# A fused attention and gated long convolution: two weight chunks moved ahead of two value tiles, and another order of work

## The chip, the cores and the metric

The kernel runs on one core of a Trainium2 chip. The metric is the device time of one execution in microseconds (us). Five executions of the kernel before took 173.39 to 174.32 us, median 173.7 us. One further execution was recorded by the hardware profiler; its numbers are the "profile" below.

The engines of the core are named as the profile names them: PE (the matrix engine, with PEld for its weight loads), DVE (VectorE), ACT (ScalarE), POOL (GpSimd) and SP (SyncE). Here POOL and SP do little but issue transfers, each in its own queue.

## The reference, cut to what matters

```python
def _attn_ref(q, k, v, n_global, n_local):           # 4 x 8 heads x 768 x 64, n_global 8, n_local 96
    scores = scale * np.matmul(q, k.transpose(0, 1, 3, 2))
    keep = is_global | is_local                      # the first 8 keys, or the last 96 positions
    scores = scores - slopes[:, None, None] * dist   # slopes 2 ** -(h + 1)
    scores = np.where(keep, scores, -1000000000.0)
    a = np.exp(scores - np.max(scores, axis=-1, keepdims=True))
    return np.matmul(a / (np.sum(a, axis=-1, keepdims=True) + 1e-09), v)

def _moe_ref(x, w_proj, filter_fft, w_out):          # x: 4 x 768 x 512, the attention's output
    proj = x @ w_proj                                # 512 x 1536
    x1, x2, x3 = (proj[..., :D], proj[..., D:2 * D], proj[..., 2 * D:])
    X2 = np.fft.rfft(x2, n=S, axis=1)
    H = np.fft.rfft(filter_fft, n=S, axis=0)[None, :, :]
    x2_conv = np.fft.irfft(X2 * H, n=S, axis=1)
    return (x1 * x2_conv * x3) @ w_out
```

Inputs and output are float32; the work is done in 16-bit types.

## The kernel before

**The work of one batch.** Attention is done in seven key tiles of 120 rows, collected in three groups `c` (tiles 0-1, 2-3, 4-6), with the eight heads in four pairs `hp`, and the pairs in two halves `j`. `scores` (L963) makes one PE group per pair and group; ACT turns it into `E` with an exponential (L1000). In batch 0 the bias and the mask are added by extra matmuls; in batches 1 to 3 DVE multiplies by a mask (L1007). `values` (L1010) multiplies `E` by the value tiles `vn`; DVE takes the reciprocal of the sums and scales the result into `xn`. `transpose_x` (L1059) turns `xn` by PE and copies it to `xT`. `values(j, 2)` needs the value tiles 3 to 6, those of the groups before it only lower ones. `gate` (L1098) makes x1 and x3 for one quarter of the 512 columns and one half `s` of the rows: two groups of four matmuls each, named w0 to w3 (x1) and w8 to w11 (x3) by their column block of `w_proj`. The half `s=0` needs `xT` of the groups 0 and 1 only; `s=1` needs group 2.

The convolution over 768 positions is split by hand into small transforms. `butterfly` (L1077) sums and subtracts thirds of `xT` on DVE, `proj` (L1169) multiplies them by the x2 columns, `spectra` (L1271) and `forward` (L915) transform the results, DVE multiplies by the filter's spectrum, PE does the inverse (L1191), DVE joins the parts (`mixed`, `gated`) and multiplies by x1*x3 to `y`, and `project` (L1219) multiplies by `w_out`. The result is evacuated into one of six buffers `ot` and stored by SP. Before the first convolution the tables of the transform and the filter's spectrum `h` are made too (`tables`, `spectrum`).

**What sets the order.** The kernel records all operations in a `Plan`, with a cost per engine and what each reads and writes. `lay` (L156) is a list scheduler in Python: of the operations that can start first it takes the one of lowest rank. The rank is the batch's due time, plus a bias, plus a noise number read from `NUDGES`, one per operation. An operation that ACT or DVE may do is given to the engine whose finish, by these costs, is earlier, after a lean has been added on DVE's side: `FAVOUR` plus a second number of `NUDGES`. So an entry of `NUDGES` can change both where an operation stands and who does it.

```python
e, s = min(((e, max(at, free[e])) for e in o.cost),
           key=lambda x: (x[1] + o.cost[x[0]] + o.lean * (x[0] == "V"), x[0]))
```

The costs serve only to fix the order. On the chip each engine works through its own list in that order, and semaphores make it wait for what it needs. Where the plan has a gap on PE, `fill` puts idle matmuls there (`busy`, L561) on a bank that is free.

**Transfers.** POOL issues all loads of q, k, v, `w_proj`, the filter and `w_out`, in the order of the recorded loads. For batch 0 `load_first` (L1313) issues the pairs of heads of q and k, then the seven value tiles, then `w_proj` in five chunks, then the filter:

```python
WL = None, None, None, [(0, 256), (1024, 256), (256, 256), (1280, 256), (512, 512)]
...
for t in range(7):
    self.load_run(("vn", 0), vt, self.v, t, 1)
for o in self.WL[3]:
    self.load_w(*o)
```

A chunk is named by its first column: w0 holds x1 of the blocks 0 and 1, w1024 x3 of the same, w256 and w1280 those of the blocks 2 and 3, w512 all of x2. The first pair of heads is loaded by SP in float32 into two buffers used later for something else (`ot` and `h1`, in `load_pair`, L600 to L616) and cast to 16 bits from there.

Of the kernel before, what the change touches and what calls it, by code (L numbers as in the profile page):

```python
# [64 lines left out]
class Plan:  # L65
# [90 lines left out]
    def lay(self):  # L156
# [84 lines left out]
        -20469, -15907, -15519, -41330, 21271, -19125, 0, -18788, -21220, 6002, 0, -7189, -43575, -36799,  # L241
        -6571, -28916, -3333, 19757, 53969, -12046, 3924, 2362, -27887, 22407, 12912, 8466, 24818, 892,
        -43717, 690, 23057, -7424, 0, -18348, 0, 12132, 0, 3318, 0, 307, 0, 10665, -36412, 26238, -3364,
        -7981, 0, 19285, 0, -5291, 0, -3358, -40138, 46, 0, 4893, -20410, 607, -3897, 25935, 14236, -472,
        -26253, 50953, -18333, -20987, 21604, -2252, -14900, -32001, -12177, 7553, 28609, 17506, -3743,
        -23847, 42942, 14917, 23914, 13863, -24322, 6302, -15137, -1614, -4820, -17466, 50019, 19029,
        -20858, -16941, -5845, 16570, 18752, -3067, 4401, 8349, 30366, -26959, 2604, 7945, 41591, -12869, 0,
        6221, 0, 17527, 0, -11888, 0, -33773, 0, -20135, 0, 31381, 0, 9598, 0, 342, 0, 5902, 0, 21318, 0,
        -31048, 0, 3779, 0, 7500, -33102, -3367, 7292, 574, -14517, -22474, 40989, -11563, -11866, -18943,
        21835, -13606, -7933, -12166, -5061, 14482, -66705, -16499, -72333, -45183, 18666, 14455, -1721,  # L250
        -14094, 21975, -16214, -38799, 11592, -32806, -4486, 58753, 1604, 32067, 9824, 58288, -8039, -6267,
        -7799, -30465, 16245, 29129, 47615, 14049, 20581, 7542, 9071, -14063, 1398, -21731, 17235, 5237,
        -5501, -11743, 11491, -6405, -6106, -51905, 13315, -17948, 16276, 5723, 510, -57089, 50036, 18885,
        10758, 3744, 17086, -20876, -6224, -59669, 34319, 11575, -10851, -49437, 16614, 3748, -6997, -23517,
        -741, -9617, -2158, -25727, 15549, -42179, 2206, 15498, 22052, 14638, 31730, -36475, -366, -1041,
        483, -60527, 26470, -25753, 48694, -36466, 4435, 25064, 15798, -2003, 880, 41085, 8640, 19549,
        -13373, 62494, -20031, -35301, -365, -10682, 12515, -39995, 9179, -44839, 20791, 21607, 12677,
        -8056, 11463, -7753, 23778, -7196, -828, 9869, 42664, -4575, 5499, -21685, -1123, 58706, -13769,
        1071, 15224, 31737, 4557, -51402, 30473, 10683, 37011, -21708, -22082, -18146, 13758, 35600, -13459,
        13377, 42708, 8338, 10228, -2747, -44553, -22549, 2967, -13095, -1261, -20387, 7291, -5928, 8626,  # L260
        -3903, -15574, 7036, -15402, -21901, 5357, -4808, 8631, -43985, -23660, 52225, -23, -37277, 3239,
        4765, 25180, -24965, -30489, -48437, 1398, 17933, -10027, 3345, -14007, -42685, -274, -8683, 11605,
        -32563, -13448, 31461, 27188, 5094, 5241, 42373, 5599, -31270, 5970, 9726, -15345, 27804, 10360,
        12837, -37873, 40504, 5471, 45899, 30654, -30112, -11882, 6890, -10173, 11360, -20642, 71457, -7037,
        37670, 35836, 15212, -3001, -161, -21054, 29167, -19964, -4626, 33026, -65921, 5985, -58627, -537,
        15188, 27998, -9214, -10266, -12514, 5532, -31329, -13816, -42538, -361, 42096, 9128, -53101,
        -24252, 36726, -6808, -39007, -15537, -38689, -36629, -7459, 13790, -6734, 1466, -11773, 3029,
        -61137, -5278, -32143, -4629, -16151, 28035, -11602, -28288, -20732, -10425, -9594, -25686, 22828,
        7308, 10617, 8409, -34612, 6321, 5099, 10385, -16522, -10028, 17262, -3342, 364, -17974, -61950,
        6074, 1677, -2070, 22933, -10718, 4341, -9076, -14027, -7023, -49231, 39984, 41324, -15930, 87908,  # L270
        29952, 30259, -1085, 17673, 22547, 65315, 11679, 71123, -10221, 17535, 4265, 30002, 38971, 52458,
        17154, 19646, 7993, -19925, 6995, 21573, 7611, 16678, 19381, -3732, -949, 89358, 14752, 32456,
        22564, 38857, 8243, 38484, 4106, 43844, 16240, 18442, 24005, 52322, -701, 54120, 10351, 816, -1700,
        36760, 14579, 12398, 35622, -18870, 13272, -8238, 15305, -14220, 3173, -10015, -12163, 21169, 18317,
        43800, 33470, -15626, -25950, 6510, 17663, 41448, -25293, -2107, 3876, 28549, 11063, 32221, 7491,
        20524, -12468, 39460, 3459, 30644, 28397, -32823, -23657, 9318, -14232, 4503, 30321, -4786, 9073, 0,
        47530, 0, 14649, 0, -6931, 0, 10167, 0, -22564, 27505, 17477, 0, -21831, -18775, 29130, 12351,
        -11426, 0, -23648, 0, -498, 0, -18653, 0, 20206, 0, -14460, 0, 5069, 0, -5644, 0, 17568, 0, -28141,
        0, -393, 0, -13744, 0, -23077, 0, 27342, 0, -17530, 0, 24883, -5429, -15687, 22286, 6382, -7868,
        14844, 27493, 22854, -7734, -7159, 20555, 20588, -3284, -9355, 45908, 26090, -1576, 10937, -27579,  # L280
        -21718, -32176, 45033, -3052, -19219, 33129, 27434, -1137, -11810, -13329, -2566, 2545, 4486,
        -15611, -1075, 9151, 352, -14471, 31815, -23667, -3395, 32969, -1271, 12653, 1976, 23324, -5368,
        -47352, 15491, 4886, 9690, 3559, 14583, 29188, 2353, 34301, 4910, 19200, -11179, 62728, 26450, 2457,
        -13343, 34676, 8057, -18974, -12923, -16321, -14742, 3933, 10896, -19278, 10205, 17364, -10269,
        16177, 35168, -20658, -11589, 43724, 41480, 24103, 858, 9853, 10552, 1525, -3996, -5471, 25781,
        30000, 2124, -2069, 21452, 930, 8726, 90512, 29611, -16321, -22500, 9310, 12752, 2100, 1887, -64324,
        -32791, -10156, 1195, -8986, 20032, 2698, -22611, 3783, -1678, 18174, -28792, -28897, -1554, 44027,
        3299, -48940, 4565, -18590, -16364, 3358, -7004, -1749, -3117, -99997, -7283, -11740, -961, 12244,
        3976, -41870, -15548, -14790, 16082, 20959, 12982, -28661, -9869, 11604, 34716, 7633, 8897, -35715,
        -33194, -11677, 21392, 27263, 20593, -24154, -8400, -33341, 33983, -5328, 3810, 16086, -23990,  # L290
        -15413, 7796, -4785, -18200, -31986, 960, -8033, 20448, 12322, -12111, -5519, -1954, -30857, -23631,
        -49557, 32119, 2870, 4580, 13819, 10505, -65607, 37080, -32639, 43079, -11814, -10582, -35676, 9162,
        -17164, 18890, 8216, -36193, -26951, 3373, 10331, 33775, -22565, 15472, -54239, 4898, -13691, 13051,
        -24460, -38679, -31280, 19957, -34749, -14184, -69485, 11274, -14610, 9461, -34260, -29091, -21709,
        4639, -33219, -22319, -3581, -7139, -39876, 6787, -24586, 5081, -42957, -1465, -27268, 9928, -4824,
        -17860, -169, 11077, -20251, -14350, -25650, -7777, -20347, -3087, -8322, -2652, -48544, 20664,
        14762, 7765, -10126, 19322, -23675, 4226, 11745, 30618, 32208, -9638, -8303, 36652, -29682, 30605,
        25183, 11602, -45023, -3073, -43350, 3788, 21530, -3684, 5619, 16323, 20467, -3647, -39265, -5491,
        15159, 41421, -297, -35005, -11635, 37570, 16744, 13685, -87265, -25114, -42709, 8456, 7722, 28568,
        -3185, 13842, -35570, -14192, -71432, 21444, -47221, 9901, -6749, 34734, -34034, -11044, -8316,  # L300
        11170, -28676, -32859, -34562, -939, 13358, 23643, 15304, -17172, -88783, -24885, 8065, -8836,
        -28589, -7133, 51761, 13875, 591, 14268, -43206, -24391, -7422, -4922, 21228, 29607, 21694, 11407,
        40731, 2375, 15358, 4701, 4274, 2370, 26735, -7772, 17616, 28130, -16612, 38345, 20779, 47960,
# [83 lines left out]
        -26478, 16518, -6769, 14702, -36704, 7115, 25920, 20180, 6584, 24513, -34083, -10775, 67709, 7241,  # L387
        -13530, 10640, 11149, 3389,
    )
    FAVOUR = -0.1  # L390

    def fill(self, out):

# [75 lines left out]
class Fused:  # L469
# [843 lines left out]
    def load_first(self):  # L1313
# [9 lines left out]
        for t in range(7):  # L1323
            self.load_run(("vn", 0), vt, self.v, t, 1)
# [102 lines left out]
```

## Time and profile before

| | before |
|---|---|
| median of five executions | 173.7 us (173.39 to 174.32) |
| the profiled execution | 173.47 us |
| its span, first to last instruction | 171.7 us |
| what lies around the span | 1.77 us |
| granted PE clock, mean | 0.995 |
| busy: PE / DVE / ACT / POOL | 164.4 / 151.1 / 150.3 / 75.5 us |
| first gate starts on PE | 26.91 us |
| ACT's last three copies into `ot` | 167.05 to 168.31 us |

A row of the profile that lists a group of instructions gives the line, the engine, the operation, what it writes and reads with the tile's shape, and the count. "Busy" of PE includes the time that its pipeline holds matmuls, so it is not a measure of the work left. A row of a timeline begins with the start and the duration. A window's row gives for each engine the busy time within the window and, in parentheses, the number of instructions. In the chain of waits each piece is the step that the next one waited for.

### The profile page before, as it was taken

Reading aid. Unit: us, or ns where it says so; the run is one execution under the profiler, and the core shown is the slowest. Engines: PE = TensorE matmul, PEld = TensorE weight load, DVE = VectorE, ACT = ScalarE, POOL = GpSimd, SP = SyncE. Lnnn points to the kernel's source line nnn. Section 1 sums busy time; section 2 is a strip of 40 time slices with the busy share of each in tenths; the row PEclk is TensorE's granted clock in tenths of the full one; section 3 lists DMA queues with packets and bytes.
Section 4 is the critical chain, followed back from the end, with each engine's and each line's share of the span. In section 5 each row is a group of like instructions: output and inputs, shape, how many; then the busy total and the mean of one; then the engine's idle time right before and its main releaser. Section 6 shows DMA issues by size and latency. Waiting matters only on the chain.

```text
span 171.7 us, 4500 instructions
## 1 busy us (share of the span) xinstructions
PE 164.4 (96%) x1727; PEld 102.5 (60%) x1727; DVE 151.1 (88%) x362; ACT 150.3 (88%) x307; POOL 75.5 (44%) x97
## 2 busy tenths in 40 slices
PE   7999899999998999999999999999999999999991
PEld 2485786656445666975446758654567774557540
DVE  6534889899999999999998999999999999999940
ACT  8999996988999799999988897989979997968762
POOL 7999876278998999999920000000000000000000
PEclk9999999999999999999999999999999999999998
DMA  5999999999999999999999995000072000043144
GB/s 178 157 127 133 128 196 207 182 150 146 129 142 169 146 148 155 144 135 159 141 133 196 239 201 114 11 0 0 0 287 83 6 2 0 4 183 124 61 181 185
DMA packets 86997, 21.82 MB, mean 127 GB/s; under 512 B 77616, under 2 KB 84032, under 8 KB 86976
## 3 DMA queue, kind: packets, MB, share of 16 engines
q0 software_dynamic: 75408, 12.47, 108.6%
q1 hardware_dynamic: 11568, 9.07, 21.2%
q8 instruction: 13, 0.21, 0.6%
q14 instruction: 8, 0.07, 0.2%
HBM read 25.69 MB, written 6.29 MB: 186 GB/s over the span
## 4 chain that ended last, share of the span: by engine, by line
PE 68%; DVE 16%; POOL 5%; DMA 4%; ACT 3%; issue 2%; POOLq 0%
PE bank L1108 19%; PE bank L1225 12%; PE bank L1169 9%; PE bank L1191 5%; PE bank L985 4%; PE bank L921 4%; DMA vn<-in_v_dram 4%; PE bank L1025 4%; PE bank L1070 3%; PE bank L1030 3%; DVE E L1007 2%; DVE xn L1049 1%; PE bank L976 1%; PE bank L935 1%; POOL kn L581 1%
## 5 line engine op out<-in xcount | busy, mean ns | idle before, releaser
L1108 PE MATMUL bank<-xT,w 128*128 128x384 f16 x256 | 44.1, 326 | 0.0
L1000 ACT ACTIVATE E<-bank 128x864 f16<-128x864 f32 x48 | 39.9, 904 | 2.5 <-PE bank L985 2.3
L1108 PEld LDWEIGHTS <-w 128*128 128x128 f16 x256 | 24.5, 98 | 16.1 <-issue 0.2
L581 POOL DMA_DIRECT2D vn<-in_v_dram x29 | 26.0, 912 | 2.2 <-DMA w<-in_moe_w_proj_dram 2.1
L1225 PE MATMUL bank<-wo,y 128*128 128x512 f16 (+1 forms) x100 | 22.3, 371 | 0.0
L581 POOL DMA_DIRECT2D kn<-in_k_dram x24 | 21.6, 906 | 1.0 <-DMA qn<-in_q_dram 0.4
L581 POOL DMA_DIRECT2D qn<-in_q_dram x21 | 18.9, 907 | 6.5 <-PE bank L1108 3.2
L1007 DVE TENSOR_TENSOR E<-E,mask 128x864 f16<-128x864 f16 x36 | 20.3, 600 | 0.3 <-ACT E L1000 0.3
L1049 DVE TENSOR_TENSOR xn<-bank,rc 128x512 f16<-128x512 f32 (+1 forms) x23 | 17.4, 763 | 0.3
L1118 ACT CAST g<-bank 128x384 f16<-128x384 f32 x32 | 15.8, 515 | 2.0 <-PE bank L1108 1.7
L569 ACT ACTIVATE ot<-bank 128x512 f32<-128x512 f32 (+1 forms) x23 | 12.8, 592 | 5.0 <-PE bank L1225 5.0
L1025 PE MATMUL bank<-vn,E 128*128 128x65 f16 x224 | 15.8, 193 | 1.1 <-DVE xn L1049 0.5
L569 ACT ACTIVATE x<-bank 128x384 f16<-128x384 f32 x28 | 14.3, 522 | 2.7 <-PE bank L1108 2.1
L1025 PEld LDWEIGHTS <-E 128*128 128x128 f16 x224 | 14.1, 97 | 2.5 <-ACT E L1000 0.3
L1225 PEld LDWEIGHTS <-y 128*128 128x128 f16 x100 | 9.3, 98 | 10.2 <-DVE y L1267 0.6
L985 PE MATMUL bank<-QT,KT 64*128 64x216 f16 (+2 forms) x224 | 14.6, 241 | 0.8 <-DVE KT L565 0.5
L1030 PE MATMUL bank<-vn,E 128*128 128x65 f16 x192 | 15.3, 193 | 0.0
L1030 PEld LDWEIGHTS <-E 128*128 128x128 f16 x192 | 13.2, 97 | 1.8 <-issue 1.4
L569 ACT ACTIVATE ab<-bank 128x512 f16<-128x512 f32 x21 | 12.5, 618 | 1.8 <-PE bank L1169 1.5
L985 PEld LDWEIGHTS <-KT 64*128 64x128 f16 x224 | 8.8, 94 | 6.5 <-issue 3.8
L565 ACT CAST X<-bank 128x512 f16<-128x512 f32 x22 | 12.4, 609 | 0.1
L565 ACT CAST eo<-bank 128x384 f16<-128x384 f32 x28 | 12.0, 550 | 0.5 <-PE bank L1194 0.2
(145 smaller groups left out, 345.7 us busy)
## 6 DMA issues: line engine op xcount, KB each, us to landing
out_dram<-ot SPq DMA_DIRECT2D x23, 256.0 KB
vn<-in_v_dram POOLq DMA_DIRECT2D x28, 120.0 KB, 6.8
kn<-in_k_dram POOLq DMA_DIRECT2D x21, 120.0 KB, 6.2
qn<-in_q_dram POOLq DMA_DIRECT2D x18, 128.0 KB, 6.6
w<-in_moe_w_proj_dram POOLq DMA_DIRECT2D x4, 256.0 KB, 8.0
g<-in_moe_filter_fft_dram POOLq DMA_DIRECT2D x1, 768.0 KB, 13.1
qn<-in_q_dram POOLq DMA_DIRECT2D x3, 192.0 KB, 4.2
kn<-in_k_dram POOLq DMA_DIRECT2D x3, 192.0 KB, 5.6
```

The source lines that it names most:

```text
L565: {"A": nc.scalar.copy, "V": nc.vector.tensor_copy, "G": nc.gpsimd.tensor_copy}[e](out, in_)
L569: self.nc.scalar.mul(out, in_, c)
L581: return self.g.op(eng, 0.57 + 0.00035 * min(nbytes[0], 1024) if eng == "G" else 0.5, lambda _: e.dma_start(dst, src), w=w, r=r, nbytes=nb ...
L985: nc.tensor.matmul(bs[hh].f32()[:, off:off + w], self.KT[hs, hp, P * m:P * m + P], self.QT[hs, hp, KL * m:KL * m + w], start=(off == 0 and ...
L1000: g.op("A", act(864), lambda _: nc.scalar.activation(eo, bs[0].two()[:, :, 0:432].rearrange("p h (m w) -> p h m w", m=2), Act.Exp, scale=s ...
L1007: g.op("V", dve(864, 2), lambda _: nc.vector.tensor_mul(eo, eo, mk), r=[("E", hp, gi), ("mask", hp)], w=[("E", hp, gi)], name="masked")
L1025: nc.tensor.matmul(o[:, n, hh], ef[:, at:at + P], vt[:, t, 2 * hp + hh, :], start=first, stop=(t == 0), skip_group_check=True)
L1030: nc.tensor.matmul(o[:, n, hh], ef[:, at:at + P], vt[:, t - 1, 2 * hp + hh, :], start=False, stop=True, skip_group_check=True)
L1049: nc.vector.tensor_mul(to, o[:, :, :, 0:D], rc.to_broadcast([P, 2, 2 * nt, D]))
L1108: nc.tensor.matmul(bk.f32()[:, 0:h], self.w[:, c, o + P * j:o + P * j + P], self.xT[:, c, h * s:h * s + h], start=(c == 0), stop=(c == 3))
L1118: g.op("A", act(h), lambda _: nc.scalar.copy(x3, pts[1].f32()[:, 0:h]), use=[pts[1]], w=[ko], name="x3")
L1225: nc.tensor.matmul(bk.f32()[:, 0:n], y[:, c, P * t:P * t + P], self.wo[:, c, cs], start=(c == 0), stop=(c == 3))
```

## The change

Four edits are made together.

1. `EARLY = 5`: the chunks w0 and w1024 are issued before the value tiles 5 and 6 of batch 0, not behind them. The other three chunks stay behind tile 6.
2. `NUDGES` is replaced: 2003 of its 2088 numbers differ. It is not printed; what it does to the order is told below.
3. `FAVOUR` goes from -0.1 to 0.0.
4. The cast in `load_pair` is recorded as reading four of the `ot` buffers, not two.

```diff
     NUDGES = (
...
     )
-    FAVOUR = -0.1
+    FAVOUR = 0.0
...
     HARD = 1
+    EARLY = 5
     WL = None, None, None, [(0, 256), (1024, 256), (256, 256), (1280, 256), (512, 512)]
...
-                r=[("stage", what, hp), ("ot", 0), ("ot", 1)], w=[(what + "n", "pair", hp)], name="cast")
+                r=[("stage", what, hp)] + [("ot", i) for i in range(4)], w=[(what + "n", "pair", hp)], name="cast")
...
         for t in range(7):
+            if t == self.EARLY:
+                for o in self.WL[3][0:2]:
+                    self.load_w(*o)
             self.load_run(("vn", 0), vt, self.v, t, 1)
-        for o in self.WL[3]:
+        for o in self.WL[3][2:]:
             self.load_w(*o)
```

What the two programs' orders show side by side:

- The operations are the same, but for the idle matmuls (27 before, 24 after).
- PE, start of the program: the eight gates of batch 0 with `s=0` come in the order w9, w8, w3, w10, w1, w2, w0, w11 before, then `transpose_x(0, 2)`, `transpose_x(1, 2)`. After, it is w9, w1, w0, w10, w2, `transpose_x(0, 2)`, a group of the tables, w3, `transpose_x(1, 2)`, w11, w8. In both, all other attention work of batch 0 stands ahead of the first gate; after, the two groups `values(0, 2)` and `values(1, 2)` stand right in front of it, and the last scores of pair 3 behind `values(1, 1)`.
- PE, later: half of batch 0's inverse transforms are spread among gates of batch 1. At the end ten gates of batch 3 stand ahead of the last seven output groups, not eight.
- DVE and ACT: DVE makes one more 768-wide `xn` in batch 0 (before, ACT did it in twelve small steps), three more copies of q's transposes and two more x1; ACT makes three more `ab`, one more `eo`, and two more `ot`, while the two halves of the very last output are evacuated by DVE. By the programs' lists DVE has 367 instructions in place of 364, ACT 295 in place of 309.
- POOL: w0 and w1024 stand ahead of the value tiles 5 and 6; among the loads of batch 3 six change places. SP: the stage of q is issued before that of k, and the transposing transfers of batch 3's q and k come in another order among the stores. The counts are the same.

## The prediction

> **What bounds the kernel now.** I read the page first: engine totals, slices, the groups of loads.
>
> ```profile
> span 171.7 us, 4500 instructions
> PE 164.4 (96%) x1727; PEld 102.5 (60%) x1727; DVE 151.1 (88%) x362; ACT 150.3 (88%) x307; POOL 75.5 (44%) x97
> ...
> PE   7999899999998999999999999999999999999991
> DVE  6534889899999999999998999999999999999940
> ACT  8999996988999799999988897989979997968762
> PEclk9999999999999999999999999999999999999998
> ...
> vn<-in_v_dram POOLq DMA_DIRECT2D x28, 120.0 KB, 6.8
> w<-in_moe_w_proj_dram POOLq DMA_DIRECT2D x4, 256.0 KB, 8.0
> ```
>
> PE looks full everywhere, but 96% is no measure of PE's need: matmuls overlap in it. From start-to-start times inside gap-free runs (163 ns for a 384-column matmul, 216 for 512, 56 for 128, 30 for 65) all of PE's work without idle matmuls adds up to 151.3 us. The last matmul ends at 167.9, so PE loses 16.6 us. Subtracting the summed work from the time at which a group starts tells where: 11.4 us are lost by the first gate (26.91); 14.85 by the first inverse (66.6); 15.9 by `transpose_x(0,1)` of batch 2 (96.8); and only 0.5 after it. So the time is made in the first 67 us. The windows and the timeline show by whom.
>
> ```profile
> 13.00:27.00 14.00, 13.31 (x264) 10.15 (x260) 10.10 (x34) 12.86 (x24) 12.07 (x15) 1.00 2.59 158
> 27.00:33.70 6.70, 6.70 (x55) 4.30 (x55) 6.14 (x15) 5.78 (x12) 2.72 (x3) 1.00 1.47 195
> 33.70:48.00 14.30, 13.55 (x109) 7.87 (x107) 13.95 (x36) 12.88 (x26) 11.65 (x13) 1.00 2.42 143
> 48.00:67.70 19.70, 18.83 (x204) 11.38 (x204) 19.39 (x49) 18.09 (x34) 18.45 (x22) 1.00 2.28 152
> 97.00:150.00 53.00, 53.00 (x526) 33.24 (x523) 51.90 (x105) 47.65 (x100) 0.00 (x0) 1.00 0.27 59
> ```
> ```profile
> 10.30 6.33 POOL L581 DMA_DIRECT2D vn<-in_v_dram  x7
> 16.59 2.32 POOL L581 DMA_DIRECT2D w<-in_moe_w_proj_dram  x3
> 19.82 4.02 ACT L1000 ACTIVATE E<-bank 128x864 f16<-128x864 f32 x5
> 33.02 0.45 DVE L565 COPY xT<-bank 128x576 f16<-128x576 f16 x1
> ```
>
> The columns of a window are the engines PE, PEld, DVE, ACT, POOL. Up to 24 us ACT sets the pace: it works without a gap, and its exponentials end at 23.84. From 33.7 to 67.7 DVE is full (13.95 of 14.30, 19.39 of 19.70), PE is not. The chain of waits agrees: PE up to the last gate of `s=0`, then DVE.
>
> ```profile
> 26.97 5.31 PE bank L1108 x32
> 32.28 0.67 PE bank L1070 x12
> ...
> 33.94 0.59 PE bank L1108 x4
> 34.54 0.39 ACT inr L569
> 34.95 0.29 DVE inv L571
> 35.25 0.46 DVE xab L1084
> ```
>
> After `xT` of group 2 is copied (33.47) DVE starts the butterflies and has a backlog until 67. DVE has done 24.1 us of work at 33.4 (sum of its instructions in order), so it has been idle for 9.3 us; at 66.7 for 9.8. Whatever lets DVE do more before 33 moves the whole stretch.
>
> **The change part by part.**
>
> *The early weights.* The semaphores in the trace give the landings: value tiles 4, 5, 6 at 21.14, 22.46, 23.30, then w0 23.76 and w1024 25.09. The first gate started at 26.91, so neither chunk was awaited (1.8 us to spare): w0 and w1024 earlier gain nothing. They cost the value tiles two places. With the landing distances of the queue, about 1.2 us a value tile and 1.3 a chunk, the new landings are w0 22.4, w1024 23.7, tile 5 24.6, tile 6 25.1 to 25.6 (the four together carry the same bytes, and their end was 25.09). `values(·,2)` waits for tile 6; before it was there at 23.3.
>
> Here a rule stands against the row. The Trainium skill, page "DMA: Bandwidth & Descriptors", section "Anatomy of one DMA — SWDGE (gpsimd) path", gives 2.0 us plus bytes over 436 GB/s for one transfer: 2.6 us for 256 KB. By it tile 6, issued near 17.4, would land by 20, and the early chunks would delay nobody. The row above has 8.0 us from issue to landing: the transfers wait for one another in the queue. The measurement decides: value tiles come 2 us later. By the rule `values(·,2)` would wait for the exponential alone; since that comes at the same time (next step), the sum is the same, but rival C would have no ground.
>
> *ACT's order ahead of the first gate.* The last exponential of group 2 now has more ACT work ahead: two masks (0.5), two table pieces (1.0), one `xT` (0.5) and one q copy less (-0.7). 23.84 + 1.3 = 25.1, up to 25.6 with waits. So exponential and tile 6 are there together at 25.1 to 25.6. Behind them stand `values(0,2)` and `values(1,2)` at 0.73 each: first gate at 27.1, against 26.91: **+0.2 us** for PE. The issue of POOL is no bound: chunk and tile merely change places (0.9 us each), and what follows them is issued at the same time. SP's swap of two stages at 0.74 and 1.26 moves two casts by up to 0.5 us, on DVE and ACT both; I take 0, because ACT's first exponentials stand behind more than these, and keep ±0.3.
>
> *Idle matmuls.* Of six idle matmuls between 10 and 27 us (five in a row) three are left, one at a time. The clock rule in "TensorE: Matmul & The Clock Gate", "Part 1: The HAM clock gate", would halve the rate after an idle window of 3.4 us. The row PEclk shows 9 in every slice, and PE's longest waits here were 0.7 us; I estimate 1.5 us at most now. By the row the fillers cost 0. By the rule it is 0 too unless a wait doubles; then up to 1.7 us, a stage's matmuls at half rate, of which ACT hides most. I take 0.
>
> *DVE before 33 us.* In the new order `xT(1,2)` is the last copy the butterflies need. It stands behind `transpose_x(1,2)`, which ends six gates, a table group and two turns after the first gate starts: 27.1 + 6x0.65 + 0.67 + 0.34 + 0.42 = 32.4, copied by 32.95. (Before: 33.47.) By then DVE's list has 25.7 us of work in it, not 24.1: a q pair (+0.87), the first two butterfly sums (+0.94) and more `xT` copies (+0.68) stand ahead now, one x1 (-0.56) and one g (-0.27) behind. So DVE's idle total is 33.0 - 25.7 = 7.3 us in place of 9.3: a **lead of 2.0 us**. It holds only if DVE is not late on the way: from `values(1,2)` on, 2.9 us of its work fill 4.6 us, so PE, not DVE, sets this end.
>
> *What takes part of it back.* In the saturated stretch PE now needs DVE to be further along. For each PE group I took the DVE work that must be done before it, less the PE work before it. The worst before is 1.4 us (first inverse: 56.9 of DVE, 55.6 of PE). After, it is 2.2 to 2.5: `values(1,1)` of batch 1 (47.5 against 45.0), inverse (55.2, 53.0), `proj` (69.3, 67.1), `transpose_x(0,1)` of batch 2 (87.5, 85.1). That is +1.1. The sum at the last of these: DVE work 87.54, its idle 7.3 plus the 0.5 that it idled in this stretch before (9.3 to 9.8), and 0.15 for the semaphore and the turn: 95.4. The same PE group stood at 96.4. Behind it is the same PE work, 71.5 us, in which DVE is 2 us ahead of need. **Sum: -1.0 us.**
>
> *Later edits.* Ten gates instead of eight before the last seven outputs: PE work is equal; DVE's last two `y` products are needed at 151.2 and 153.8 of PE work and ready at 150.5 and 153.4, so 0. The last output's halves go from ACT to DVE (0.38 each on ACT, DVE is idle there): 0, ±0.2. Six loads of batch 3 and its thirteen transposing transfers change places; the closest tile still lands 1.5 us before its use: 0. The cast's wider dependence concerns `ot` buffers first used after 80 us: 0. `FAVOUR` acts through the placements counted above alone.
>
> The profiled execution had 173.47 (span 171.7 and 1.77 around it), 0.2 below the median of 173.7. Against the median: 173.7 - 1.0 = **172.7**.
>
> **The rivals.** Under 0.5% (0.87 us) a measurement of this kernel cannot tell a change from none.
>
> *A: the lead is kept* (above): 172.7, and 171.9 if DVE idles no more at all. For it: windows with DVE full from 33.7. Chance 0.46.
>
> *B: DVE waits for ACT, and the lead leaks.* ACT has 18.09 busy of 19.70 in the fourth window, and the three `ab` and several exponentials there stand before DVE's work. Walking both lists by hand, DVE's idle grows by 0.9, not 0.5: 95.8, or -0.6; a few semaphores more make it -0.2. 173.1 to 173.6. Chance 0.26.
>
> *C: slower; the value tiles decide.* One mechanism: the two chunks hold tile 6 back, both `values(·,2)` wait for it at the head of PE's list, and the eight gates and all of DVE's butterflies stand behind them. Then DVE's idle total is not 7.3 but grows one for one with tile 6, while the +1.1 of further need stays. The sum is 0 when `xT(1,2)` ends at 34.0, that is tile 6 (or the last exponential) at 26.6; with it at 27.6 the kernel is 1.0 slower: 174.7; at 28.1, 175.2. For it: a late queue, 2.59 mean DMA share in this window with its last chunk at 30.77. Against it: the same bytes were through by 25.09. The same loss results if DVE is late there through ACT. Chance 0.28.
>
> *D: it does not do what it says.* That no gate waited for w0 or w1024 (25.09 against 26.91) is certain by the trace; so the early load alone is worth 0 or less, and all gain comes from the order. This is inside A to C.
>
> **How the numbers follow.** Faster 0.46 (A), same 0.26 (B), slower 0.28 (C). Likeliest 172.7; A's own range is 171.6 to 172.8. The range for all: from 171.6 (A with the ±0.3 of the stages in its favour) to 175.2 (C with tile 6 at 28.1), which leaves out about 0.07 below and 0.11 above.
>
> **What would show each step.** The value tiles 5 and 6 land at 24.6 and 25.1 to 25.6 and w1024 by 24; the first gate starts at 27.1 +- 0.4; the last copy of `xT` (group 2) ends near 33.0 and DVE's idle total there is 7.3; `transpose_x(0,1)` of batch 2 starts near 95.4; the span is 170.7; PEclk stays at 9. I am wrong if a gate starts after 28, if DVE's idle total between 33 and 67 grows by over 1.5 us, or if PE stalls again after 97.

## The result and the profile after

The changed kernel takes 172.83 us (median of 43 executions, 172.37 to 174.57) against 174.11 us for the kernel before (78 executions, 172.88 to 176.32). The medians are 1.3 us apart; the ratio of the two kernels is 0.9938 with a 95% interval of 0.9924 to 0.9951, so 1.1 us or 0.6% faster. All ratios leave out the few executions that lie more than 1.5% above the fastest of their kernel. The forecast was 172.7. The profiled executions stand nearer together: 172.83 (span 171.1) after, 173.47 (span 171.7) before, a difference of 0.64. The one before was a fast one among its 78; the larger sample also puts the median of before 0.4 above the five executions that the forecast started from.

The page of the changed kernel:

```profile
span 171.1 us, 4493 instructions
PE 163.4 (96%) x1724; PEld 101.0 (59%) x1724; DVE 153.0 (89%) x365; ACT 147.4 (86%) x293; POOL 75.5 (44%) x97
```

DVE has 1.9 us more work than before and ACT 2.9 us less. That matters below. The timeline of POOL, ACT and DVE at the start (start, duration, engine and line, what, count; in brackets the idle time before and who ended it):

```profile
15.02 1.54 POOL L584 DMA_DIRECT2D w<-in_moe_w_proj_dram  x2
16.55 1.93 POOL L584 DMA_DIRECT2D vn<-in_v_dram  x2
...
25.50 0.89 ACT L1003 ACTIVATE E<-bank 128x864 f16<-128x864 f32 x1 [0.28 <-PE bank L988]
...
31.31 0.46 DVE L568 COPY xT<-bank 128x576 f16<-128x576 f16 x1 [0.44 <-PE bank L1073]
32.97 0.46 DVE L568 COPY xT<-bank 128x576 f16<-128x576 f16 x1
```

The chunks are issued ahead of the value tiles 5 and 6. By the semaphores they land at 21.96 and 23.69, the tiles at 24.72 and 25.56. The last exponential of group 2 ends at 26.39. The first gate starts at 27.52. Both `xT` of group 2 are copied by 33.43, the first of them by 31.77. Before, DVE copied the first at 33.02 and ACT the other, and both were there by 33.73.

The windows of the saturated stretch, columns as in the prediction:

```profile
33.70:48.00 14.30, 13.53 (x108) 7.73 (x106) 14.20 (x36) 12.97 (x26) 13.01 (x15) 1.00 2.35 148
48.00:67.70 19.70, 19.52 (x234) 11.89 (x232) 19.25 (x47) 18.42 (x33) 17.59 (x20) 1.00 2.33 150
```

DVE is as full as before, but PE is now too: it is busy for 19.52 of 19.70 us in the second window, where it had 18.83. The chain of waits says the same. Before, it ran over DVE from 35 to 67; after, it leaves DVE at 45.7 and runs mainly over projections and transforms on PE up to 57 (start, duration, what):

```profile
43.70 0.69 DVE pp L868
44.65 0.50 DVE g L872
...
45.71 1.02 PE bank L924 x4
47.68 0.97 PE bank L1172 x4
50.03 0.86 PE bank L1172 x4
```

To see where time is won, I took each PE group's start less the PE work that stands ahead of it in the list: the time that PE has lost so far, called its idle total here. The durations are taken group by group from the trace of before, so small stalls inside groups count as work, and the totals are lower than in the prediction; an instruction that lasts longer than in that trace counts as idle time. The same was done for DVE. Only differences between kernels count.

| profiled execution | first gate | DVE idle at 33.5 | PE idle at first gate | PE idle at 150 | span |
|---|---|---|---|---|---|
| before | 26.91 | 9.3 | 9.7 | 11.3 | 171.7 |
| after | 27.52 | 7.6 | 10.4 | 10.8 | 171.1 |
| after, once more (e11) | 27.38 | 7.5 | 10.2 | 10.7 | 171.0 |
| e1 after, old queue | 27.91 | 8.0 | 10.7 | 11.4 | 171.7 |
| e2 before, new queue | 29.36 | 11.7 | 12.2 | 13.7 | 174.1 |
| e5 after, th1 later | 27.27 | 7.4 | 10.1 | 10.8 | 171.1 |
| e10 th1 later, old queue | 27.28 | 7.4 | 10.1 | 10.4 | 170.7 |
| e6 after, turns late | 27.48 | 10.1 | 10.3 | 13.2 | 173.5 |
| e3 after, DVE +1.8 | 27.28 | 9.3 | 10.1 | 14.3 | 174.6 |
| e4 before, DVE +1.8 | 26.68 | 11.0 | 9.5 | 13.4 | 173.8 |
| e12 before, q2 and turns | 26.51 | 7.6 | 9.3 | 11.4 | 171.8 |

The kernel before lost 1.6 us of PE time behind the first gate; the changed one loses 0.4 there, after starting the gates 0.6 later.

### The profile page after: what moved, and what is told of

Same layout as the page of the kernel before. It is cut to its first block, busy times and chain, and to the rows that moved or that the text cites. A ratio compares the mean times of both kernels' runs of the same rounds, so it can differ in the third digit from the quotient of the medians.

```text
span 171.1 us, 4493 instructions
## 1 busy us (share of the span) xinstructions
PE 163.4 (96%) x1724; PEld 101.0 (59%) x1724; DVE 153.0 (89%) x365; ACT 147.4 (86%) x293; POOL 75.5 (44%) x97
## 4 chain that ended last, share of the span: by engine, by line
PE 71%; DVE 14%; ACT 11%; issue 2%; ACTq 0%
PE bank L1111 18%; PE bank L1228 12%; PE bank L1172 11%; PE bank L924 6%; PE bank L1194 5%; PE bank L988 4%; ACT E L1003 4%; PE bank L1028 3%; PE bank L1073 3%; PE bank L1033 3%; PE bank L938 2%; ACT slope L572 2%; ACT mask L834 2%; ACT near L568 1%; DVE g L1123 1%
## 5 line engine op out<-in xcount | busy, mean ns | idle before, releaser
L1111 PE MATMUL bank<-xT,w 128*128 128x384 f16 x256 | 45.6, 326 | 0.2 <-DVE x L574 0.2
L1003 ACT ACTIVATE E<-bank 128x864 f16<-128x864 f32 x48 | 41.1, 913 | 1.0 <-PE bank L988 0.8
L1010 DVE TENSOR_TENSOR E<-E,mask 128x864 f16<-128x864 f16 x36 | 21.0, 598 | 0.3 <-ACT E L1003 0.3
L1052 DVE TENSOR_TENSOR xn<-bank,rc 128x512 f16<-128x512 f32 (+1 forms) x24 | 18.3, 769 | 0.2
L572 ACT ACTIVATE ab<-bank 128x512 f16<-128x512 f32 x24 | 14.8, 617 | 2.7 <-PE bank L1172 2.5
L572 ACT ACTIVATE ot<-bank 128x512 f32<-128x512 f32 x23 | 13.4, 611 | 4.3 <-PE bank L1228 4.2
L1228 PEld LDWEIGHTS <-y 128*128 128x128 f16 x100 | 9.6, 98 | 10.4
L572 ACT ACTIVATE x<-bank 128x384 f16<-128x384 f32 x26 | 13.0, 507 | 2.7 <-PE bank L1111 2.2
L568 ACT CAST eo<-bank 128x384 f16<-128x384 f32 x29 | 12.9, 504 | 2.0 <-PE bank L1197 1.9
L1033 PEld LDWEIGHTS <-E 128*128 128x128 f16 x192 | 13.2, 97 | 0.7
L988 PEld LDWEIGHTS <-KT 64*128 64x128 f16 x224 | 8.3, 94 | 7.1 <-issue 4.8
```

The source lines that it names most:

```text
L568: {"A": nc.scalar.copy, "V": nc.vector.tensor_copy, "G": nc.gpsimd.tensor_copy}[e](out, in_)
L572: self.nc.scalar.mul(out, in_, c)
L988: nc.tensor.matmul(bs[hh].f32()[:, off:off + w], self.KT[hs, hp, P * m:P * m + P], self.QT[hs, hp, KL * m:KL * m + w], start=(off == 0 and ...
L1003: g.op("A", act(864), lambda _: nc.scalar.activation(eo, bs[0].two()[:, :, 0:432].rearrange("p h (m w) -> p h m w", m=2), Act.Exp, scale=s ...
L1010: g.op("V", dve(864, 2), lambda _: nc.vector.tensor_mul(eo, eo, mk), r=[("E", hp, gi), ("mask", hp)], w=[("E", hp, gi)], name="masked")
L1033: nc.tensor.matmul(o[:, n, hh], ef[:, at:at + P], vt[:, t - 1, 2 * hp + hh, :], start=False, stop=True, skip_group_check=True)
```

## The experiments

Line numbers of the experiments' profiles are shifted, since each adds a few lines. In the edits `line[e]` is the list of operations of an engine, after the plan is made and before it is written out; banks stay as the plan gave them. Ratios are to the kernel before, on the same chip.

**e1: the early weights undone.** In the changed kernel, POOL's list alone is put back:

```diff
+w = [find("G", x) for x in ("w0", "w1024")]
+v = find("G", "load('vn', 0)6")
+for o in w:
+    line["G"].remove(o)
+line["G"][line["G"].index(v) + 1:line["G"].index(v) + 1] = w
```

> The changed kernel with one thing undone: POOL issues value tiles 5 and 6 ahead of w0 and w1024 again; every other instruction stands where the change put it. Theory A (the gain is the order of work: DVE starts the butterflies earlier; the weights were never awaited): no difference to the changed kernel, within 0.3 us; tile 6 lands near 23.3 and w1024 near 25.1, and the first gate stays at 27.5, because values(0,2) stands behind transpose_x(1,1), which waits for xn(1,1) (end 25.78), not for tile 6 (25.56). Rival B (the early weights bring the gain): back to the time of before, +1.1 us.

172.82 us (nine executions), ratio 0.9932 (0.9902 to 0.9962): the changed kernel's own. Tile 6 landed at 24.77 in the profile (the queue was late in this execution, with tile 4 at 21.96 against 21.24), w1024 at 26.55. The first gate at 27.91 came behind 0.24 us in which PE waited for nothing that the profile shows. The early weights are worth nothing in the new order.

**e2: the early weights alone.** The same edit the other way round, in the kernel before:

```diff
+v = [find("G", "load('vn', 0)%d" % t) for t in (5, 6)]
+w = find("G", "w1024")
+for o in v:
+    line["G"].remove(o)
+line["G"][line["G"].index(w) + 1:line["G"].index(w) + 1] = v
```

> The kernel before with the early weights alone: POOL issues w0 and w1024 ahead of the value tiles 5 and 6, all else as before. Theory A: slower. values(1,2) started at 23.89, tile 6 now lands near 25.5, so values(1,2) starts 1.7 us later, and the first gate moves from 26.9 to 28.0 to 28.6; DVE's start of the butterflies moves with it, so the end is 0.9 to 1.7 us later than before. Rival B (early weights bring the gain): about 1 us faster than before. Rival C (the transfers have slack): within 0.3 us of before.

176.26 us (median of six), ratio 1.0126 (1.0077 to 1.0174): 2.2 us slower. Part of that is the clock: three of the six executions took 176.5 to 179.1 us with a mean granted clock of 0.978 to 0.988, the other three, at 0.996 to 1.0, took 175.3 to 176.1, which is 1.1 to 1.9 above the 174.2 of the kernel before on this chip. The profiled one had 1.0. In it tile 6 landed at 26.44, 3.1 us later than before, not the 2.2 I expected. Its waits between 20 and 30 us (engine, line, for whom: total, times, longest):

```profile
PE bank L1042 <- DMA vn<-in_v_dram: 1.5, 2, 0.9
```

`values(1,2)` starts at 24.57, stops twice for tiles 5 and 6 and ends at 27.25, in place of 24.79; the first gate comes 2.45 us later, and the span is 2.4 us longer. So the mechanism of rival C is real in an order that reads tile 6 early: what the first gate loses, the span loses. The changed kernel escapes it since it puts both `values(·,2)` last.

**e5: what held the first gate.** In the changed kernel one VectorE instruction changes place:

```diff
+move("V", find("V", "", ("th", 1)), find("V", "xn", ("xn", 1, 1)), 1)
```

> The changed kernel with one VectorE instruction moved: the table piece th1 (24.70 to 25.19, ahead of xn(1,1)) goes behind xn(1,1). Theory A1 (the first gate came at 27.5 and not at 27.1 because xn(1,1) was late on DVE): xn(1,1), transpose_x(1,1) and both values groups come 0.4 us earlier, the first gate at 27.1 to 27.2, and the end is 0.3 to 0.4 us earlier. Rival A2 (tile 6 at 25.56 or the last exponential at 26.40 held the gate): 0 to -0.1 us.

The first gate came at 27.27, 0.25 earlier in the profile. The median was 172.64 (172.41 to 172.95), ratio 0.9917 (0.9887 to 0.9946): it looks 0.2 to 0.4 faster than the changed kernel, but the intervals overlap. The PE idle total stays 0.25 lower up to 40 us and is back at the changed kernel's value by 64. So the first theory is right about the hold, `xn(1,1)`, though only 0.25 of the 0.4 us came; in this profile even that is given back later.

**e6: the turns behind all gates again.** In the changed kernel, on PE only:

```diff
+gate = [o for o in line["P"] if o.name == "gate"][7]
+for o in [o for o in line["P"] if o.name == "trx"][4:6][::-1]:
+    move("P", o, gate, 1)
```

> The changed kernel with one thing undone on PE: transpose_x(0,2) and (1,2) stand behind all eight gates of s=0 again, as before, instead of among them. PE's work and the order on all other engines stay. Theory A (DVE's earlier start of the butterflies is the gain): xT(0,2) is copied near 33.9 instead of 31.8, xT(1,2) near 34.4 instead of 33.4, DVE's idle total there grows by 1.9 to 2.2 us, and the end is about 2 us later. Rival D (the gain is in PE's later order, the inverse groups spread among gates, and needs no lead of DVE): within 0.3 us of the changed kernel.

176.8 us (median of six), ratio 1.016 (1.0111 to 1.0209). DVE's timeline:

```profile
33.89 0.46 DVE L583 COPY xT<-bank 128x576 f16<-128x576 f16 x1 [2.71 <-PE bank L1088]
...
35.47 0.45 DVE L583 COPY xT<-bank 128x576 f16<-128x576 f16 x1
```

DVE waits 2.71 us for the turn, its idle total is 2.5 us higher, and in the profile PE's idle total ends 2.4 higher (span 173.5 against 171.1). That is one for one. The median is later still: three of the six executions took 177.3 to 178.0 us with a mean granted clock of 0.99, the others 175.3 to 176.3 at 0.998 to 1.0. What such a clock means is seen in e3.

**e3 and e4: DVE delayed, in both kernels.** Fourteen memsets of a small tile stand right behind a copy of `xT` of group 2, `xT(1,2)` in the changed kernel and `xT(0,2)` in the one before:

```diff
+def probing(self):
+    for _ in range(14):
+        self.nc.vector.memset(self.spare, 0.0)      # 128 x 32, 16 bit
```

> The changed kernel with extra work on VectorE: 14 small memsets (about 0.06 us each, 0.85 us in all) right behind the copy of xT(1,2) that ended at 33.43, so ahead of most butterflies. Nothing waits for them. Theory A (after 33 us DVE sets the end, so the lead counts one for one): 0.6 to 0.9 us later than the changed kernel. Rival D (DVE has slack after the change and PE alone sets the end): 0 to 0.2 us.

> The kernel before with the same 0.85 us of small memsets right behind the copy of xT(0,2) that ended at 33.47. Theory A: the chain of waits runs over DVE from 35 to 67, so 0.6 to 0.9 us later than before. Rival D: 0 to 0.2 us.

The delay was twice what I meant:

```profile
33.13 1.77 DVE L580 MEMSET spare<- 128x16 uint32 x13
```

e4: 175.87 us, ratio 1.0079 (1.0047 to 1.011), 1.4 us slower; in the profile DVE's idle total (the memsets count as idle) is 1.65 higher at 33.5 and PE's 2.1 higher at the end. e3: 175.78 us, ratio 1.007 (1.0033 to 1.0107). So the changed order without its lead (DVE idle total 9.3, as in the kernel before) is slower than the kernel before, by 1.2 us. In its profile PE's idle total ends 3.5 higher for 1.65 of delay. Two windows tell why (the number behind POOL's is the granted clock):

```profile
44.44:47.85 3.41, 2.00 (x25) 1.28 (x26) 3.34 (x8) 3.40 (x4) 3.41 (x5) 1.00 2.35 146
47.85:51.26 3.41, 3.41 (x15) 1.22 (x14) 3.23 (x7) 0.59 (x2) 3.41 (x4) 0.50 2.44 152
```

PE waited for DVE several times between 42 and 47.7; then its clock was halved for 3.41 us, and a 512-column matmul took 0.43 us from start to start in place of 0.22. That costs 3.41 x 0.5 = 1.7 us, nearly all that e3 lost in this profile beyond the delay itself.

Which of the seven executions had such a stretch follows from their mean clock, for one stretch takes 1.7 of 174.6 us, or 0.01, off the mean. The three at 0.988 or 0.989 took 176.4 us. The one at 1.0 took 174.4 and the three at 0.997 took 175.3 to 175.8: too little clock is missing there for such a stretch. In all the other kept traces the clock falls only behind the last matmul, where it costs nothing. In the kernel before, with a mean of 0.995, the last matmul ends at 167.89:

```profile
167.90:170.00 2.10, 0.00 (x0) 0.00 (x0) 0.00 (x0) 0.40 (x2) 0.00 (x0) 1.00 0.88 326
170.00:171.70 1.70, 0.00 (x0) 0.00 (x0) 0.00 (x0) 0.00 (x0) 0.00 (x0) 0.51 0.00 0
```

So four executions of e3 lost nothing to the clock. Their median is 175.5, still 1.2 us behind the kernel before on the same chip (174.31), and by an estimate 2.2 behind the changed kernel (0.9938 x 174.31 = 173.2) for 1.65 of delay.

**e9 and e12: parts of the change put into the kernel before.** e9 gives one copy, of q's pair 2, to DVE; e12 adds the early turns and the first butterfly sums:

```diff
+q2 = find("A", "qT", ("QTp", 2))                   # e9 and e12
+line["A"].remove(q2)
+q2.eng = "V"
+line["V"].insert(max(i for i, o in enumerate(line["V"]) if ("KTp", 1) in o.wk) + 1, q2)
+move("P", trx[4], gate[5], 0)                      # e12 only
+move("P", trx[5], gate[6], 1)
+move("V", find("V", "xT", ("xT", 0, 2)), g, 1)     # g: the first g on DVE
+move("V", a, x, 1)                                 # a, b: sums xa, xb of j = 0; x: that copy
+move("V", b, a, 1)
```

> The kernel before with one part of the change alone: the copy of q's turned pair 2 goes from ACT (11.53 to 12.35) to DVE, which idled from 10.62 to 15.38. Theory A (the lead is DVE work done in early idle time, and ACT set the first stage): ACT's exponentials come up to 0.7 us earlier, DVE's idle total at 33.5 falls from 9.3 by what the first gate gains, and the end is 0.3 to 0.7 us earlier than before. Rival H (the first stage of before is held by its own chain of value tiles and xn, so the place of this copy alone changes nothing): within 0.2 us.

> The kernel before with two parts of the change: q's pair 2 copied by DVE, and transpose_x(0,2) and (1,2) placed among the last three gates of s=0, with the copy of xT(0,2) and the first two butterfly sums behind the first g on DVE. Theory A (DVE's place at 33 us decides, whatever order follows): DVE's idle total at 33.5 falls from 9.3 to 8.2 to 8.8, and the end is 0.5 to 1.1 us earlier than before, about as the changed kernel. Rival D (the later order decides): within 0.3 us of before.

e9: ratio 1.001 (0.9977 to 1.0042). Its profile is no good witness: inside `values(1,2)` PE stands still for 0.9 us (24.3 to 25.2), waiting for nothing that the profile shows. e12: 174.06 us, ratio 0.9996 (0.9971 to 1.0021), so no gain, although DVE's idle total at 33.5 is that of the changed kernel. The copy of `xT(0,2)` starts at 30.91 in place of 33.02. The chain of e12:

```profile
33.54 5.20 PE bank L1134 x32
...
47.55 0.60 DVE ab L597
```

The same step `ab` in the chain of the kernel before:

```profile
47.75 0.60 DVE ab L571
```

Up to 42 us the chain of e12 runs over PE's gates and first projections, in the old order, and the DVE step `ab` comes 0.2 us earlier, no more. Of the 1.7 us of lower idle total 0.9 is the copy itself, work that DVE did not have before. The rest is not used: the chain shows no place where the old order gets anything from DVE earlier than by those 0.2 us. So DVE's lead is needed (e3, e6) but is not the gain; the later order (rival D of e6 and e12) has its share.

**e7 and e8: resorted lists.** Both take the changed kernel with the old queue and give each engine a list of operation numbers, worked out from the old traces:

```diff
+def edit(line):
+    for e, text in ORDER.items():
+        by, idle = {o.n: o for o in line[e] if o.n >= 0}, [o for o in line[e] if o.n < 0]
+        line[e][:] = [by[int(x)] if x != "i" else idle.pop(0) for x in text.split()]
```

> A version meant to be faster than both: the changed kernel, the tiles 5 and 6 ahead of the weights again, and the lists of PE, ACT and DVE resorted by hand within the first 90 us (about 107, 107 and 149 places differ) so that fewer instructions wait; same operations on the same engines, same idle matmuls. Theory F (the 10.4 us that PE idles ahead of the first gate still hold about 1 us, and DVE can follow): first gate near 26.6, xT(1,2) copied by 31, end 0.7 to 1.3 us earlier than the changed kernel. Rival G (as with th1: what is won ahead of the gates is given back by DVE between 40 and 62): 0 to -0.3 us. Also possible: the new order has waits that cannot be seen in the old traces, and it is slower.

> As the resorted version, but only instructions of the first 34 us change places (32 on PE, 57 on ACT, 51 on DVE); what comes later stays as in the changed kernel. Theory F: first gate near 26.0 to 26.6, butterflies of the first half ahead of the x1 copies, end 0.6 to 1.2 us earlier than the changed kernel. Rival G: 0 to -0.3 us, the PE idle total being back at 10.7 by 64 us.

Both are slower than the changed kernel: e7 took 176.16 us (ratio 1.0113, 1.0077 to 1.0148), e8 175.19 us (1.0034, 1.0000 to 1.0068, so hardly to be told from the kernel before). e8 lost at the start. The memset of the tile that the idle matmuls read had moved back on DVE:

```profile
2.48 5.50 PE L581 MATMUL bank<-idle 128*128 128x512 f16 x18 [2.48 <-DVE idle L694]
```

They began at 2.48, not 1.20, and the first exponential came 0.7 later (14.07 against 13.33). The first gate came at 27.51, as in the changed kernel, but the third only at 29.61, not 28.82, behind one more group of values, and the second `xT` of group 2 was copied by 35.03, not 33.43. e7 had its first gate at 27.16 and its DVE idle total at 7.2, both better than the changed kernel, and lost 3.9 us of PE time between 36 and 90. A better start is no gain in an order that then waits.

**e10 and e11: the best version, beside the changed kernel again.** e10 has the edits of e1 and e5 together; e11 is the changed kernel unaltered.

> The changed kernel with th1 behind xn(1,1) and the tiles 5 and 6 ahead of the weights again. Theory A: the two edits hold no common wait, so it is like the run with th1 alone, first gate near 27.3, 0.1 to 0.4 us faster than the changed kernel. Rival C (tile 6, landing within half a microsecond of its use, costs time in executions with a slow queue): 0.5 us or more faster, and a smaller spread.

> The changed kernel once more, on the same chip as the others of this set, as what they are held against. All theories: 0.9938 of the kernel before, that is about 1.1 us faster.

e11: 173.01 us (172.42 to 173.62), ratio 0.993 (0.9902 to 0.9958). e10: 172.62 us (172.24 to 172.85), ratio 0.9908 (0.9878 to 0.9938). e10 has the lowest ratio of all, 1.6 us below the kernel before; that it beats the changed kernel is likely but not shown (0.4 us, intervals overlap). Its spread of 0.6 us against 1.2 fits rival C's remark on slow queues; six and seven executions are few.

## Why the prediction was right, and where its steps were off

Size and direction were right: -1.1 measured, -1.0 forecast. The mechanism was right only in part. DVE's lead came and is needed, but it is not where the gain comes from; and that 172.7 lay so near 172.83 is partly luck, as the steps show:

- *Weights not awaited; early weights worth nothing.* Shown by e1. Landings were forecast as 22.4, 23.7, 24.6 and 25.1 to 25.6, and were 21.96, 23.69, 24.72 and 25.56. By the formula of the Trainium skill ("DMA: Bandwidth & Descriptors", "Anatomy of one DMA — SWDGE (gpsimd) path"), which is for one transfer, tile 6 would have been there by 20; it was right to prefer the trace, and e2 shows what the two places in the queue cost where the tile is awaited.
- *First gate at 27.1.* It was 27.52, 27.38 in e11. The step that failed is the start of `values(0,2)`, put at 25.1 to 25.6 because tile 6 and the last exponential were taken for what it waits for. It started at 26.23. The exponential was late too: from "23.84 + 1.3", ACT alone, it was to end at 25.1 to 25.6 and ended at 26.39, with waits of ACT for PE of 0.43 and 0.28 us in front of it. But `values(0,2)` had begun by then. The chain to it runs over DVE's `xn` and the turns of PE:

```profile
23.98 0.70 DVE xn L1052
...
25.84 0.40 PE bank L1073 x4
26.23 0.03 PE bank L1028
```

The turn at 25.84 needs `xn(1,1)`, which ended at 25.78; e5 moved one instruction from in front of that and won 0.25. DVE was late because it had begun the `xn` ahead of these at 23.15 only, after a wait that an exponential ended. The waits of the changed kernel from 13 to 28 us begin with it:

```profile
DVE rc L1057 <- ACT E L1003: 2.3, 1, 2.3
```

ACT waited for PE, PE for DVE and DVE for ACT, and a sum over one engine misses such a ring.
- *DVE's idle total 7.3 in place of 9.3.* It was 7.6. It hangs on the turns among the gates: with them behind the gates (e6) the total is 2.5 higher.
- *"Whatever lets DVE do more before 33 moves the whole stretch."* This inference failed. Downward it holds: e4, e6 and, with a clock loss on top, e3. Upward it does not: e12. As I read it, the sum survived because its other term, the +1.1 for PE needing DVE further along, was taken from the new lists and holds the added DVE work. e3 tests that term: with the lead gone, rival C's text has the changed order 1.1 us behind the kernel before. The four executions of e3 that lost no clock are 1.2 behind by their median, but they spread over 1.4 us, so the term is supported, not measured.
- *DVE's idle grows by 0.5 in the stretch.* By the same sums it grew by 0.9 (7.6 to 8.5 at 60), the figure of rival B. But that is no leak through waits: by the windows above DVE is without work for only 0.10 + 0.45 = 0.55 us from 33.7 to 67.7, before for 0.35 + 0.31 = 0.66.
- *95.4 in place of 96.4.* The sum itself is 87.54 + 7.3 + 0.5 + 0.15 = 95.49, so about -0.9; and 96.4 is not the start of that group, which is 96.84 in the trace, but the time in the kernel before at which 71.5 us are left to the end of the last matmul. `transpose_x(0,1)` of batch 2 started at 95.90; the span is 171.1, not 170.7. Against the profiled execution of before, the sum was 0.36 too hopeful. Against the medians the gain was 0.3 too small (1.0 for 1.3) and the base of 173.7 was 0.4 too low, and these two nearly cancel in 172.7.
- *The tail at 0.* From the end of the last matmul to the end of the span it is 3.8 us in both (167.89 to 171.7, 167.27 to 171.1).
- *Fillers at 0.* The clock stayed at 1.00 in all windows up to 150 us. The fillers were not tried alone, nor was `FAVOUR`.

What is left open: which of the later moves bring PE's loss behind the first gate from 1.6 to 0.4 us. The candidates seen in the chain are the projections and transforms of 45 to 57 us. No run takes them apart.

## What to carry to other kernels

A lead on a saturated engine is worth something only if the order behind it uses the lead, and an "idle total" falls also when work is added; compare the time of one and the same step instead (47.75 and 47.55 in e12). Where a weight load moves up a queue, look first for what it moves back: here the weights gained nothing and the later value tiles cost about 2 us in an order that reads them early. A sum against one profiled execution should say how far that execution lies from the median, for that was as large an error as any step (0.64 us here).

## What the runs showed of the hardware that I had not expected

- The matrix engine's clock fell to half without any long idle time: in e3 PE was busy 1.47, 1.49 and 0.65 us in the three windows of 2 us from 42 to 48, and ran at 0.50 from 47.85 to 51.26. "TensorE: Matmul & The Clock Gate" of the Trainium skill, "Part 1: The HAM clock gate", names an idle window of about 3.4 us as the cause; here the single waits of the matmuls before the drop were 0.86, 0.66 and 0.73 us. A low busy share alone does not do it either: PE was busy 2.00 of the 3.41 us before the drop, and in e2 1.95 of the 3.41 us from 24.00 on, where the clock stayed at 1.00. What sets it off stays open.
- In all the kept traces, each stretch at one clock lasts a whole multiple of 3.41 us, save the last, which the end of the record cuts: 12, 1 and 36 times 3.41 us in e3, 48 in the kernel before, 49 in the changed one.
- Small instructions in a row start farther apart than they last: each of the fourteen memsets of 128x16 words took 0.07 us, but they started 0.14 us apart. I had sized the delay of e3 and e4 from the 0.06 us that a lone 1x2 one took at the start of the program, so it was twice as large as meant.
- The landing time of the seventh value tile, in the same place of the queue, was 23.25, 23.30 and 24.77 us in three profiles (e9, before, e1), and PE can stand still for up to 0.9 us with no cause in the trace (e9). Both are as large as the change.
